# PSUM banks in two halves, first sums evacuated ahead, low-rank product by column halves, and another order of the first loads

One Trainium2 chip, one core. The metric is the device time of that core in microseconds (us): the median of several executions, of which most agree within 0.3%. The span of a trace is about 1.75 us shorter than the time of the same execution (the traced run of the kernel before took 699.6 us and has a span of 697.8), so times are compared with times and spans with spans.

## The reference, cut

```python
def _attn_ref(q, k, v, lam):                     # (4, 8, 768, 64), float32
    for b in range(nb):                          # blocks of the sequence
        intra = (q k^T * decay mask) v           # within the block
        inter = (q * lam^(pos+1)) kv_state       # from earlier blocks
        out[block] = intra + inter
        kv_state = lam^block * kv_state + (k * lam^(block-1-pos))^T v

def _moe_ref(x, U, V, w_ch1, w_ch2):             # x: (4, 768, 512)
    h = x.transpose(0, 2, 1) @ U @ V             # rank 32, mixes tokens
    u = x + h.transpose(0, 2, 1)
    return u + relu(u @ w_ch1) @ w_ch2           # 512 -> 2048 -> 512
```

## The kernel before

The attention runs in 24 steps of 128 tokens (six for each of four batches); `x_nat` is its result, tokens on partitions. When the six steps of a batch are done, `low` and `low_sum` form its low-rank part, `mix` adds it (`pu`), and `turn` transposes the sum (`put`), splits it into parts for the later products, and sends the sum to DRAM (`u_d`; one of the parts has the same name). The tiles with p are PSUM tiles: within a step, `pq` and `pk` hold the transposed q and k, `pss` the scores, `px` the weighted v, `pkv` the new state, `pxn` the transposed result; `pp` and `pr` belong to the low-rank product. Each is emptied by an instruction on ScalarE or VectorE (the copies `qt`, `kt`, `xt`, `x_nat`, for instance), and the program gives its bank to the next tile only after that. `mask` holds the powers of the decays by which the scores are multiplied (`sm`). In the head, the first units of products, the last `mix` and `turn` pieces stand between the products. After that come only products: `pz` takes two of the three parts of a product, `pd` the third.

```python
    x_pool = mix_ctx.enter_context(tc.tile_pool(name="x", bufs=8, side="right"))
    ...
    ps = ctx.enter_context(tc.tile_pool(name="ps", bufs=8, space=bass.MemoryType.PSUM))
    def bank(shape, name):
        return ps.tile(shape, FP32, tag="bank", name=name)      # one ring of eight banks
    ...
    def back(s):                       # end of step s: transpose the attention's result
        px = bank([P, CT, P], "pxn")
        for ct in range(CT):
            nc.tensor.transpose(out=px[:, ct, :], in_=xt[:, ct, :], identity=ident)
        xs[s] = x_pool.tile([P, C], FP32, tag="x", name="x_nat")
        nc.scalar.copy(xs[s].rearrange("p (c n) -> p c n", n=P), px)

    def low(b):                        # 12 records: column groups 0..3, then 0..1
        pp = bank([P, C], "pp")
        for c in range(NT):
            g = c % G
            nc.tensor.matmul(
                out=pp[g * R : (g + 1) * R, :], lhsT=u_w[:, c, :], rhs=xs[b * NT + c],
                start=(c < G), stop=(c + G >= NT),
            )
        pts[b] = tmp("pt")
        nc.scalar.copy(pts[b], pp)

    def mix(s):
        pu = bank([P, C], "pu")
        nc.tensor.matmul(out=pu, lhsT=v_hl[:, c * P : (c + 1) * P], rhs=p_hl, start=True, stop=True)
        nc.vector.tensor_tensor(out=xs[s], in0=pu, in1=xs[s], op=ALU.add)

    def turn(s):
        pt = bank([P, CT, P], "put")
        ...
        nc.sync.dma_start(out=u_d[s], in_=xs.pop(s))   # in the attention steps: one step later
    ...
    load_next("q")                     # step 0 in two halves each
    load_next("k", nc.scalar)
    nc.scalar.dma_start(out=lamb, in_=lam.unsqueeze(0).broadcast_to([P, H]))   # the decays
    for name in "vqkvqkv":
        load_next(name)
    ...
    def hidden(ft, pair, before={}):   # one unit of products
        ...                            # 16 pz, then 8 pd, with pieces of mix and turn between
        for g in pair:
            pz, pd = acc[g]
            r = r_pool.tile([P, N], FP32, tag="r", name="r")
            nc.scalar.mul(r, pz, 1.0 + E)
            nc.vector.scalar_tensor_tensor(r, pd, 4096.0, r, ALU.mult, ALU.add)
            nc.sync.dma_start(out=r_d[ft][g], in_=r)
```

## Time and profile before

| | |
|---|---|
| time, median of 3 (range) | 700.29 us (699.34 to 700.83) |
| span of the trace | 697.8 us |
| TensorE busy | 684.1 us, 98% |
| VectorE, ScalarE, GpSimd busy | 72%, 44%, 15% |
| moved by DMA | 131.18 MB, mean 188 GB/s |

TensorE leaves 13.7 us of the span idle. Every part of the change can only win from these or from work on TensorE before 171 us. The prediction shows the views that say where they lie.

### The profile page before, as it was taken

To read this page: it belongs to the slowest core of one execution; us is meant where nothing else is said; L and a number is where in the kernel's file an instruction comes from. 1 tells how busy PE (TensorE), PEld (TensorE's weight loads), DVE (VectorE), ACT (ScalarE), POOL (GpSimd) and SP (SyncE) were. 2 spreads that over 40 slices of the span, in tenths; PEclk is the share of its full clock that TensorE was granted. 3 is DMA by queue.
4 is the path that set the end of the run, shared out by engine and by line. 5 is a ranking of instruction groups with operands and counts; after the bars stand their busy time and mean duration, and the time that the engine had idled before them with its cause. 6 is when DMAs were issued, how large, how long until landed. Compare 5 with 4: busy or idle time off the path is not lost.

```text
span 697.8 us, 11361 instructions
## 1 busy us (share of the span) xinstructions
PE 684.1 (98%) x4176; PEld 555.3 (80%) x4176; DVE 501.5 (72%) x903; ACT 305.6 (44%) x543; POOL 108.0 (15%) x91
## 2 busy tenths in 40 slices
PE   7999999998999999999999999999999999999997
PEld 6979797966888888888888888888888888888886
DVE  4868787866899777777779435777686586776864
ACT  4777777854566544444455322232232222322320
POOL 3425554524000000000000000011030030300300
PEclk9999999999999999999999999999999999999999
DMA  9997786333477555656657889966354363363531
GB/s 196 219 200 183 181 212 166 95 101 141 170 258 250 197 203 211 209 208 209 206 204 269 288 304 366 351 193 201 96 163 150 90 212 99 122 187 90 167 92 60
DMA packets 131688, 131.18 MB, mean 188 GB/s; under 512 B 81392, under 2 KB 89584, under 8 KB 131632
## 3 DMA queue, kind: packets, MB, share of 16 engines
q1 hardware_dynamic: 130432, 130.18, 61.1%
q8 instruction: 33, 0.54, 0.3%
q10 hardware_dynamic: 1200, 0.27, 0.2%
q14 instruction: 23, 0.19, 0.1%
HBM read 80.09 MB, written 50.33 MB: 187 GB/s over the span
## 4 chain that ended last, share of the span: by engine, by line
PE 88%; DVE 4%; ACT 3%; DMA 2%; issue 1%; POOL 0%; ACTq 0%; DVEq 0%; POOLq 0%
PE pz L613 25%; PE pz L745 13%; PE pz L743 13%; PE pd L747 13%; PE pd L620 12%; PE pss L341 2%; PE px L364 2%; PE px L359 2%; DMA u_d<-x_nat 2%; PE pxn L404 1%; PE put L456 1%; PE pkv L380 1%; DVE ut L460 1%; PE pk L306 1%; PE pq L306 1%
## 5 line engine op out<-in xcount | busy, mean ns | idle before, releaser
L613 PE MATMUL pz<-u_hl,w 128*128 128x512 f32 x768 | 190.4, 398 | 0.0
L613 PEld LDWEIGHTS pz<-u_hl,w 128*128 128x128 f32 x768 | 144.5, 188 | 36.0 <-issue 1.3
L743 PE MATMUL pz<-w_hl,m 128*128 128x512 f32 x384 | 151.6, 396 | 0.0
L745 PE MATMUL pz<-w_hl,m 128*128 128x512 f32 x384 | 151.6, 396 | 0.0
L747 PE MATMUL pd<-w_d,m 128*128 128x512 f32 x384 | 150.0, 396 | 0.0
L727 ACT ACTIVATE m<-mt 128x512 fp32r<-128x512 f32 x96 | 60.7, 632 | 196.0 <-PE pd L747 138.2
L728 DVE SCALAR_TENSOR_TENSOR m<-rm,m 128x512 fp32r<-128x512 f32 x96 | 71.5, 746 | 54.3 <-ACT m L727 53.8
L628 DVE SCALAR_TENSOR_TENSOR r<-pd,r 128x512 f32<-128x512 f32 x96 | 61.9, 686 | 59.6 <-ACT r L627 52.5
L767 POOL TENSOR_TENSOR o<-o,u 128x512 f32<-128x512 f32 x20 | 29.9, 1526 | 450.7 <-DVE o L765 450.7
L620 PE MATMUL pd<-u_d,w 128*128 128x512 f32 x384 | 98.8, 397 | 0.0
L745 PEld LDWEIGHTS pz<-w_hl,m 128*128 128x128 f32 x384 | 72.3, 188 | 17.7
L747 PEld LDWEIGHTS pd<-w_d,m 128*128 128x128 f32 x384 | 72.3, 188 | 17.6
L743 PEld LDWEIGHTS pz<-w_hl,m 128*128 128x128 f32 x384 | 72.3, 188 | 17.6
L620 PEld LDWEIGHTS pd<-u_d,w 128*128 128x128 f32 x384 | 72.2, 188 | 17.4
L627 ACT ACTIVATE r<-pz 128x512 f32<-128x512 f32 x96 | 52.0, 594 | 60.8 <-PE pz L613 60.8
L729 DVE SCALAR_TENSOR_TENSOR m<-m 128x512 fp32r<-128x512 f32 x96 | 69.2, 721 | 0.9
L726 DVE TENSOR_SCALAR mt<-rm 128x512 uint32<-128x512 uint32 x96 | 46.2, 482 | 25.3 <-DMA rm<-r_d 25.0
L179 ACT CAST w<-wt 128x512 fp32r<-128x512 f32 x32 | 19.9, 622 | 40.6 <-DVE wt L176 32.4
L364 PE MATMUL px<-sm,vraw 128*64 128x128 f32 x384 | 36.1, 274 | 0.3 <-DVE sm L347 0.2
L347 DVE TENSOR_TENSOR sm<-pss,mask 128x512 f32<-128x512 f32 x48 | 30.9, 685 | 6.2 <-PE pss L341 4.3
L359 PE MATMUL px<-qs,kv 128*64 128x128 f32 x320 | 32.2, 279 | 0.0
L136 ACT ACTIVATE sc<-sc,ends 128x512 f32<-128x512 uint32 x29 | 21.0, 724 | 19.2 <-DVE sc L132 19.2
(82 smaller groups left out, 760.8 us busy)
## 6 DMA issues: line engine op xcount, KB each, us to landing
r_d<-r SPq DMA_DIRECT2D x96, 256.0 KB, 2.8
rm<-r_d SPq DMA_DIRECT2D x96, 256.0 KB, 2.7
words<-in_moe_w_ch_dram SPq DMA_DIRECT2D x32, 512.0 KB, 4.4
w_d<-w SPq DMA_DIRECT2D x16, 768.0 KB, 3.3
w_hl<-w_d SPq DMA_DIRECT2D x16, 512.0 KB, 6.1
u_d<-x_nat SPq DMA_DIRECT2D x24, 256.0 KB, 3.8
u<-u_d SPq DMA_DIRECT2D x24, 256.0 KB, 4.1
out_dram<-o SPq DMA_DIRECT2D x24, 256.0 KB, 2.0
```

The costliest lines, as they stand in the source:

```text
L364: nc.tensor.matmul(out=px[x * D : (x + 1) * D, a, :], lhsT=vr[:, 2 * a + x, :], rhs=sm[:, x, a, :], start=(c == 0), stop=True,)
L613: nc.tensor.matmul(out=acc[g][0], lhsT=w[:, n, ct, :], rhs=uhl[g][:, n, ct, :], start=(ct == 0 and n == 0), stop=(ct == CT - 1 and n == 1),)
L620: nc.tensor.matmul(out=acc[g][1], lhsT=w[:, 2, ct, :], rhs=ud[g][:, ct, :], start=(ct == 0), stop=(ct == CT - 1),)
L627: nc.scalar.mul(r, pz, 1.0 + E)
L628: nc.vector.scalar_tensor_tensor(r, pd, 4096.0, r, ALU.mult, ALU.add)
L726: nc.vector.tensor_scalar(t.bitcast(U32), r.bitcast(U32), HI, None, ALU.bitwise_and)
L727: nc.scalar.activation(out=m[:, 0], in_=t, func=AF.Relu)
L728: nc.vector.scalar_tensor_tensor(m[:, 1], r, 0.0, hi, ALU.max, ALU.subtract)
L729: nc.vector.scalar_tensor_tensor(m[:, 2], hi, E, low, ALU.mult, ALU.subtract)
L743: nc.tensor.matmul(out=pz, lhsT=m[:, 0, cols], rhs=hl[:, 0], start=first, stop=False)
L745: nc.tensor.matmul(out=pz, lhsT=m[:, 1, cols], rhs=hl[:, 1], start=False, stop=end)
L747: nc.tensor.matmul(out=pd, lhsT=m[:, 2, cols], rhs=dd, start=first, stop=end)
```

## The change

Its intent: give `pss`, `px` and `pkv` (and `pz`, `pd` in the first units) PSUM banks of their own; evacuate `pz` while `pd` is still computed; let the second round of the low-rank product use all four column groups of the array; fetch the decays before anything else and the second q and k before the first v. The diff, cut to its core:

```diff
-    def bank(shape, name):
-        return ps.tile(shape, FP32, tag="bank", name=name)
+    def bank(shape, name, tag="bank"):
+        return ps.tile(shape, FP32, tag=tag, bufs={"bank": 4}.get(tag, 2), name=name)
 # load(): v of step 0 in one piece
-        n = H // parts(s)
+        n = H if name == "v" else H // parts(s)
 # constants(): make_gather() moved here from step 4
-        pss = [bank([P, HP, P], "pss") for x in range(2)]
+        pss = [bank([P, HP, P], "pss", "pz") for x in range(2)]
-        px = bank([P, HP, P], "px")
+        px = bank([P, HP, P], "px", "pd")
-            pkv = bank([P, HP, D], "pkv")
+            pkv = bank([P, HP, D], "pkv", "pd")
 # low(): four of 512 columns, then four of 256 columns in four column groups
+        for i in range(G):
+            c, cols = G + i // 2, slice(i % 2 * half, (i % 2 + 1) * half)
+            nc.tensor.matmul(
+                out=pp[i * R : (i + 1) * R, cols], lhsT=u_w[:, c, :],
+                rhs=xs[b * NT + c][:, cols], start=False, stop=True,
+            )
 # v_steps(): two of the four ScalarE copies of vp a step earlier, two a step later
-    load_next("q")
-    load_next("k", nc.scalar)
     nc.scalar.dma_start(out=lamb, in_=lam.unsqueeze(0).broadcast_to([P, H]))
-    for name in "vqkvqkv":
+    for name, engine in (
+        ("q", nc.sync), ("k", nc.scalar), ("q", nc.sync), ("k", nc.sync), ("v", nc.scalar)
+    ):
+        load_next(name, engine)
+    for name in "vqkv":
         load_next(name)
 # hidden(): after the products pz, before the products pd
+        rs = {g: r_pool.tile([P, N], FP32, tag="r", name="r") for g in pair}
+        for g in pair:
+            nc.scalar.mul(rs[g], acc[g][0], 1.0 + E)
 ... (the weights' steps a step later, sets of pz and pd banks that alternate: cut)
```

More of the change, by code (lines that the diff above doesn't have):

```diff
@@ L264, in constants @@
         make_identity(nc, ident)
+        make_gather()
         for a in range(HP):
@@ L413, in low @@
         pp = bank([P, C], "pp")
-        for c in range(NT):
-            g = c % G
+        for c in range(G):
             nc.tensor.matmul(
-                out=pp[g * R : (g + 1) * R, :], lhsT=u_w[:, c, :], rhs=xs[b * NT + c],
-                start=(c < G), stop=(c + G >= NT),
+                out=pp[c * R : (c + 1) * R, :], lhsT=u_w[:, c, :], rhs=xs[b * NT + c],
+                start=True, stop=False,
+            )
+        half = C // 2
+        assert 2 * (NT - G) == G
+        for i in range(G):
[3 more added lines that the diff above has]
+                rhs=xs[b * NT + c][:, cols], start=False, stop=True,
             )
@@ L533, in five, with high @@
             )
-            for out, rows in parts((0, 2)):
-                nc.scalar.copy(out, t[rows])
+            high(0)
+        def high(g):
+            for out, rows in parts((g,)):
+                nc.scalar.copy(out, st["t"][rows])
         def low(g):
@@ L543, in v_steps @@
         halves = [moe_V[:, half * SH : (half + 1) * SH] for half in range(2)]
-        return weight_steps(dst, halves, SH, 2 * R) + [five, lambda: low(1), lambda: low(3)]
+        return weight_steps(dst, halves, SH, 2 * R) + [
+            five, lambda: low(1), lambda: high(2), lambda: low(3)
+        ]
     u_side = weight_steps(
@@ L553 @@
         (u_side, (-1, 2, 2, 2, 2)),
-        (v_steps(), (0, 3, 3, 4, 4, 5, 5, 6)),
-        (w1_steps(0), (3, 7, 8, 9, 10, 11, 12, 13)),
-        (w1_steps(1), (5, 14, 15, 16, 17, 18, 19, 20)),
-        (w1_2[:4], (15, 21, 22, 23)),
+        (v_steps(), (0, 3, 3, 4, 4, 4, 5, 6, 6)),
+        (w1_steps(0), (3, 7, 8, 9, 10, 12, 13, 14)),
+        (w1_steps(1), (5, 15, 16, 17, 18, 19, 20, 21)),
+        (w1_2[:3], (15, 22, 23)),
     ):
@@ L560 @@
             side.setdefault(n, []).append(step)
-    side[4].append(make_gather)
     def aside(s):
@@ L594, in enter_first_product, with banks @@
         set_ends(r_pool.tile([P, 2], FP32, tag="ends", bufs=1, name="ends"))
-    def banks():
-        return [bank([P, N], name) for name in ("pz", "pd")]
+    def banks(n, other):
+        tags = ("bank", "bank") if other else ("pz", "pd")
+        pzs, pds = ([bank([P, N], name, tag) for i in range(n)] for name, tag in zip(("pz", "pd"), tags))
+        return list(zip(pzs, pds))
+    turns = iter([0, 0, 0] + [1, 0] * (NG * FT))
     def hidden(ft, pair, before={}):
-        acc = {g: banks() for g in pair}
+        acc = dict(zip(pair, banks(len(pair), next(turns))))
         count = iter(range(12 * len(pair)))
@@ L624, in hidden @@
         for g in pair:
-            pz, pd = acc[g]
-            r = r_pool.tile([P, N], FP32, tag="r", name="r")
-            nc.scalar.mul(r, pz, 1.0 + E)
-            nc.vector.scalar_tensor_tensor(r, pd, 4096.0, r, ALU.mult, ALU.add)
-            nc.sync.dma_start(out=r_d[ft][g], in_=r)
+            nc.vector.scalar_tensor_tensor(rs[g], acc[g][1], 4096.0, rs[g], ALU.mult, ALU.add)
+            nc.sync.dma_start(out=r_d[ft][g], in_=rs[g])
     def w2_steps(ft):
@@ L679 @@
     head = [(pair, ft) for two in (pairs[:2], pairs[2:]) for ft in (0, 1) for pair in two]
-    side = list(zip((2, 3, 3, 4), w1_2[4:]))
+    side = list(zip((2, 2, 3, 3, 4), w1_2[3:]))
     for i, (pair, ft) in enumerate(head):
@@ L732 @@
     acc = {}
+    spare = next(turns)
     def product(i, n, parts=range(3)):
@@ L737, in product @@
         if ft == 0:
-            acc[n] = banks()
+            acc[n] = banks(1, n // 2 != spare)[0]
         pz, pd = acc[n]
```

## The prediction

> **What bounds the kernel now.** I read the busy row by slices first, then the chain that ended last, then the waits of TensorE, and only then the timeline in the places those three point to.
>
> ```profile
> PE   7999999998999999999999999999999999999997
> ...
> PE pz L613 25%; PE pz L745 13%; PE pz L743 13%; PE pd L747 13%; PE pd L620 12%; PE pss L341 2%; PE px L364 2%; PE px L359 2%; DMA u_d<-x_nat 2%; PE pxn L404 1%; PE put L456 1%; PE pkv L380 1%; DVE ut L460 1%; PE pk L306 1%; PE pq L306 1%
> ```
>
> TensorE is busy from end to end, and three quarters of the chain are the products pz and pd of the two matrix stages. The chain in order of time shows how full that part is:
>
> ```profile
> 171.06 3.75 PE pz L613 x16
> 174.82 1.87 PE pd L620 x8
> 176.69 3.75 PE pz L613 x16
> ```
>
> Sixteen products of 512 columns take 3.75 us, eight take 1.87: 234 ns each, without a gap, from 171 us to about 690 us. Nothing in the change removes a product there, so those 519 us cannot move; the old eight banks already hide every evacuation. Whatever the change is worth lies in 0 to 171 us and must be an idle stretch of TensorE or work taken from it. Those are:
>
> ```profile
> 1.85 4.36 DMA lamb<-in_lam_dram
> 6.30 2.65 DVE mask L268 x8
> 8.95 0.02 issue
> 8.98 0.17 DVE small L272
> 9.15 1.20 DVE sm L347 x2
> 10.35 0.04 issue
> 10.39 0.93 PE px L364 x13
> ```
>
> The start waits for the decays (lamb), not for q and k: they land at 6.2 us, then eight scans and the masking run.
>
> ```profile
> 38.38 0.66 PE L404 MATMUL pxn<-ident,xt 128*128 128x128 f32 x4 [1.18 <-ACT xt L369]
> ```
>
> One gap of 1.18 us at 38 us: the chain shows ScalarE making four copies of vp (0.52 us each, 35.65 to 37.73) ahead of xt, after VectorE spent 30.14 to 31.67 us on gather.
>
> ```profile
> 156.98 0.63 PE L456 MATMUL put<-ident,x_nat 128*128 128x128 f32 x4 [0.86 <-ACT uf L467]
> 159.88 0.63 PE L456 MATMUL put<-ident,x_nat 128*128 128x128 f32 x4 [0.41 <-ACT uf L467]
> ...
> 166.61 0.63 PE L456 MATMUL put<-ident,x_nat 128*128 128x128 f32 x4 [1.24 <-ACT uf L467]
> ...
> 169.51 0.63 PE L456 MATMUL put<-ident,x_nat 128*128 128x128 f32 x4 [0.41 <-ACT uf L467]
> ```
>
> Four gaps, 2.92 us together, where the first units of products are mixed with the last transposes. The profile blames uf, but x_nat (the addition on VectorE) ends at 156.84, 0.14 us before the transpose: the true recurrence is transpose, ut, u_d, x_nat, next transpose, 2.90 us a turn, and before 156.98 and 166.61 VectorE also did the two evacuations r.
>
> **What the Trainium skill says.**
> - Perfetto Trace Analysis, Optimizing Tensor Performance, Matmuls: groups should rotate through different PSUM banks so that evacuation overlaps the next products. The trace agrees with eight (no gap after 171 us). The change gives the attention part a rotation of four, so this is where to look for harm.
> - TensorEngine Tiling (Array Packing), Key Properties: independent tiles of the array run in parallel, and 128x32 gives four. The trace agrees: the twelve records of pp, 512 columns each, take 1.84 us in the chain, while pk, four transposes of 128 columns over the whole array in the same fp32, takes 0.44 us for those 512 columns in a pass. Twelve in a row would be 5.3 us; 1.84 is about two rounds of two passes (1.76).
> - PSUM, Terms: two engines on one bank at once are an error, reads included. The trace agrees in that uf begins 0.18 us after u_d, its neighbour on the same bank, has ended. So a bank is held until its last reader in turn.
> - DMA: Bandwidth & Descriptors, Specifications: below 512 B a transfer is not at line rate. All 12,430 packets of the first 16 us are smaller, and after a burst of up to 281 the rate stays at 204 to 222 GB/s, where later slices of the page reach 366.
>
> **The change part by part.**
>
> *Start.* The decays are asked for first, and gather moves into the time when VectorE waits for them. The mask should be done near 7 us rather than 8.95. But TensorE runs in order, and the transposes of the second q and k stand before px. In the old trace the second k is transposed at 9.02 us. Its data come fifth of five loads of 256 KB; now v of the first step goes on ScalarE's queue, but it shares the same saturated transfers, so about as many bytes precede the second k, and it lands near 8.9. px then starts near 9.5 instead of 10.39: **-0.9 us**. A third load ahead is still deep enough afterwards (5 us to land, nearly 15 us of lead).
>
> *v.* gather (1.5 us of VectorE) is gone from there, and two of the four vp copies come a step earlier, two a step later. The gap of 1.18 goes, perhaps 0.05 stays: **-1.15 us**.
>
> *Low rank.* Round two used two of the four column groups for 512 columns; now four groups take 256 columns each. It falls from 2 x 0.44 to 2 x 0.22: some 0.43 us, four times: **-1.7 us**. All four stand on TensorE's path.
>
> *First sums ahead.* The copies pz to r (2 x 0.54 on ScalarE) now run beside pd's products (1.87 us), so VectorE's r can begin when pd ends. In the old trace it begins at 153.63, with x_nat before it done at 153.00: about 0.5 us earlier, at 163.26 likewise. Two gaps shrink by 0.5 each: **-1.0 us**. The two of 0.41 stay, as they are the recurrence itself. From 171 us on: 0.
>
> *Banks.* pss, px and pkv keep banks of their own. pq, pk, pu, pxn, put (and pp, pr) share four. In a full step the order on TensorE is pxn, put, pq, pk, pu: pu is the fourth after pxn and gets its bank. The order of the changed program, with its waits, confirms it: every pu of a full step but the first waits for the copy x_nat out of pxn, and two of the four pp wait for the copy qt out of pq. The old program has no such wait. Is x_nat in time? ScalarE holds it back itself, as the buffer it fills is still being written out:
>
> ```profile
> ACT x_nat L406 <- DMA u_d<-x_nat: 8.1, 5, 2.2
> ...
> 63.35 0.48 PE L439 MATMUL pu<-vp 128*128 128x512 f32 x1
> ...
> 63.79 0.59 ACT L406 COPY x_nat<-pxn 128x512 f32<-128x512 f32 x1 [1.29 <-DMA u_d<-x_nat]
> ```
>
> Here pu started 1.03 us before x_nat ended. Over all steps, start of pu against end of x_nat: 63.35 and 64.38; 74.06 and 74.88; 93.17 and 93.97; 104.34 and 105.64; 110.03 and 111.00; 123.52 and 123.94; elsewhere x_nat is first or level. Added up 5.3 us, some 5.8 with 0.07 us for the signal. Not all of it comes: the transfer is sent off after the step's pk, so a stall of one pu gives the next transfer more time, and old waits at 108.31 (0.49) and 114.06 (0.22) are covered by it. I book 1.1 + 0.2 + 0.9 + 0.8 (104 and 110 together) + 0.35 and 0.15 of crumbs: **+3.5 us**.
>
> Sum: -0.9 - 1.15 - 1.7 - 1.0 + 3.5 = -1.25. 700.29 - 1.25 = 699.0; I put the estimate at **698.8 us**, a little lower, because the stalls shrink most easily.
>
> **The rivals.**
> 1. *The new bank wait costs nothing.* If the transfers u_d land sooner, for instance because TensorE's stalls and the other start shift them, only the gains remain: -4.75, 695.5 us. For it: most steps have x_nat level with pu within 0.1 us. Against: five waits with a median landing of 3.9 us and up to 5.1 are in the old trace, and the chain pk, issue, landing, x_nat has nothing in it that the change shortens.
> 2. *The bank wait comes in full*, the stalls not helping the next step, and pp's wait for qt eats what its halves save: +5.8 - 4.75 + 0.5, 701.8 us. For it: at 74 us pp began 0.9 us before qt ended. Against: the argument of the sent-off transfer above.
> 3. *The start does not move*, since the small packets set the landing of the second k: 0.9 us less gain, 699.7. For it: the flat rate of some 218 GB/s. Against: v, which went ahead of the second q and k, now runs beside them.
> 4. *The head gets a wait of its own*: units 0 to 2 all use one set of pz and pd banks, so unit 1 needs ScalarE's two copies done at 152.0, when its first product is due at 152.25 in the old trace. A late copy would cost some 0.3 us twice. A gain of far more than 5 us has no source: there is no more idle time before 171 us to win.
>
> **Range and chances.** The gains are each small and known to about 0.4 us, together some 0.9; the stall is known to about 2. That gives 695.8 to 701.2 for eight in ten. Two per cent are 14 us: faster than 686.3 would need more than all idle time of TensorE (13.7 us of the span, 5 of it at the end and before the first data). Faster 0.01, within 2% 0.98, slower 0.01.
>
> **What would show it right or wrong.** Right: waits of pu for x_nat near 60, 90 and 100 us, none over 1.5 us; pp groups of about 1.4 us; px of the first step near 9.5 us; no gap before pxn at the sixth step; two smaller gaps at the mixed units; 234 ns a product after that. Wrong: pu without a wait for x_nat (rival 1), pu waiting in nearly every step (rival 2), px at 10.4 (rival 3), pz of the second or third unit waiting for r (rival 4), or a product rate other than 234 ns after 171 us, which none of this foresees.

## The result, and the profile after

The changed kernel took **701.77 us** (median of 6, 700.14 to 703.87), the kernel before **700.32** (699.34 to 700.83) in the same rounds: ratio 1.002, 95% interval 1.0002 to 1.0038. By the limit of 2% that is "same". A ratio here is the mean time of one kernel's fast runs over that of the other's of the same rounds, so not quite the ratio of the medians quoted. The predicted range ended at 701.2, so the time lies above it; the class was right.

First the start. The chain that ended last, kernel after (start, length, what):

```profile
1.78 5.80 DMA kraw<-in_k_dram
7.62 0.69 PE pk L308 x2
8.31 2.01 PE pss L343 x16
10.32 0.93 PE pq L308 x4
11.69 1.07 PE px L366 x16
```

The decays no longer stand in the chain; the second half of the first k does, and px is reached at 11.69 us instead of 10.39. (In the kernel before, two of the sixteen px run at 9.80 and the rest from 10.39. A cleaner mark is the first pss of the second step: 13.18 us instead of 11.88.) The busy tenths of the 16 DMA engines and the bytes moved, in each fifth of a microsecond from 0 to 8 us, show why. Before:

```profile
DMA  0000000003658999999999999999999999999999
GB/s 0 0 0 0 0 0 0 0 0 76 145 118 204 286 287 263 271 291 264 229 224 220 220 192 181 226 219 213 222 221 215 221 216 207 219 223 220 219 218 216
```

After:

```profile
DMA  0000000003456235635799999999999999999999
GB/s 0 0 0 0 0 0 0 0 0 91 103 117 129 54 85 115 137 80 128 163 232 248 250 264 265 248 269 268 237 232 223 229 227 219 218 220 216 218 218 218
```

From 2.4 to 3.8 us, where the kernel before moves 204 to 291 GB/s, the changed one moves 54 to 137, and its DMA engines are busy for 2 to 6 tenths of the time only: they are not full.

Then the banks. The waits of TensorE, kernel after (total us, times, longest):

```profile
PE pu L449 <- ACT x_nat L408: 4.0, 3, 1.8
PE put L466 <- ACT uf L477: 2.0, 4, 0.8
PE pxn L406 <- ACT xt L371: 0.4, 1, 0.4
```

The first line has no counterpart before; there the lines (those of the first loads left out) were:

```profile
PE put L456 <- ACT uf L467: 2.9, 4, 1.2
PE pxn L404 <- ACT xt L369: 1.7, 2, 1.2
PE pr L425 <- ACT pt L421: 0.2, 1, 0.2
```

The longest of the waits of pu, and the copy that it waits for, in the timeline:

```profile
113.47 0.59 ACT L408 COPY x_nat<-pxn 128x512 f32<-128x512 f32 x1 [3.41 <-DMA u_d<-x_nat]
114.11 0.49 PE L449 MATMUL pu<-vp 128*128 128x512 f32 x1 [1.75 <-ACT x_nat L408]
```

ScalarE sat idle for 3.41 us because x_nat goes into a buffer that the DMA u_d was still reading; pu then waited 1.75 us for the bank that this copy empties. The other two waits (0.94 at 64.58 us, 1.33 at 95.69) have the same cause.

The gains are there too. One low-rank product, chain of the kernel before and then of the kernel after:

```profile
39.91 1.84 PE pp L416 x12
```

```profile
40.37 1.00 PE pp L417 x8
41.36 0.43 PE pp L426 x8
```

That is 1.84 against 1.43. The waits of put in the head fell from 2.9 to 2.0 us (0.86, 0.41, 1.24, 0.41 became 0.33, 0.40, 0.52, 0.77: the last one grew), and the gap before pxn at the sixth step from 1.18 to 0.39. From the last transposes on the same 16 products take the same 3.75 us:

```profile
173.24 3.75 PE pz L634 x16
```

### The profile page after: what moved, and what is told of

Read it like the earlier page. It is cut to its first block, busy times and chain, and to the rows that moved or that the text cites. A ratio compares the mean times of both kernels' runs of the same rounds, so it can differ in the third digit from the quotient of the medians.

```text
span 700.1 us, 11380 instructions
## 1 busy us (share of the span) xinstructions
PE 683.6 (98%) x4192; PEld 555.9 (79%) x4192; DVE 501.5 (72%) x903; ACT 305.7 (44%) x543; POOL 108.0 (15%) x91
## 4 chain that ended last, share of the span: by engine, by line
PE 91%; DMA 4%; DVE 3%; ACT 1%; issue 0%; ACTq 0%; DVEq 0%
PE pz L634 25%; PE pz L765 13%; PE pz L767 13%; PE pd L769 13%; PE pd L644 13%; PE pss L343 3%; DMA u_d<-x_nat 3%; PE px L366 2%; PE px L361 2%; PE pxn L406 1%; PE pkv L382 1%; PE put L466 1%; PE pq L308 1%; PE pk L308 1%; DMA kraw<-in_k_dram 1%; DVE sm L349 1%
```

## The experiments

Fifteen kernels ran. All outputs are right. Each batch shared a chip and its runs of the kernel before (medians 700.25, 700.01, 700.23 and 700.23 us). "After" is the changed kernel. What a part costs is read below from the difference of two ratios. Their intervals reach 0.0012 to 0.0018 to either side, so such a difference is uncertain by some 0.002, or 1.5 us (an estimate from these intervals).

### What the banks cost: one ring again, and nine buffers

e1 is after with all eight banks in one ring:

```diff
-        return ps.tile(shape, FP32, tag=tag, bufs={"bank": 4}.get(tag, 2), name=name)
+        return ps.tile(shape, FP32, tag="bank", bufs=8, name=name)
```

> The changed kernel with one ring of eight banks again, everything else kept. Theory (ring): the four-bank ring makes pu wait for the copy x_nat, 4.0 us of waits in the trace and some 4.3 us between 44 us and 142 us once the two shorter pp are counted; so this run is 4 us faster than the changed kernel, about 697.7 us and 0.996 of the kernel before, and no pu waits for x_nat. Rival (side work): the attention part is longer because weight conversions were shifted by a step and delay ScalarE; then this run stays within 1 us of 701.8 and the x_nat copies come as late as before, with TensorE waiting elsewhere for them.

Measured: 697.79 us (697.4 to 698.1), ratio to before 0.9967 (0.9955 to 0.998). No pu waits any more. By the two ratios the ring of four costs 1.002 - 0.9967 = 0.0053 of 700.3, that is 3.7 us. The same edit between e2 and e7 (both with the old start, see below) gives 0.9995 - 0.9945 = 0.0050, or 3.5 us. The rival (weights' steps that delay ScalarE) is out: those steps are the same in e1.

e3 leaves the ring of four and gives x_nat a ninth buffer. It has to take one from r, since SBUF is full otherwise:

```diff
-tc.tile_pool(name="x", bufs=8, side="right")
+tc.tile_pool(name="x", bufs=9, side="right")
-tc.tile_pool(name="r", bufs=5, reuse_waits="tile")
+tc.tile_pool(name="r", bufs=4, reuse_waits="tile")
```

> The changed kernel, four-bank ring kept, but with nine instead of eight buffers for x_nat (and four instead of five for r, to fit). Theory (ring and write-out together): x_nat then waits for a write-out issued a step earlier, so it comes at most 0.1 us after the moment at which pu wants its bank; pu's waits vanish though the ring is the same, 3 to 4 us faster than the changed kernel, about 698. Rival (ring alone): ScalarE is too late for a ring of four anyway, waits of the same length stay, time 701.8.

Measured: 697.0 us (696.41 to 697.66), 0.9958 (0.9944 to 0.9972). The waits of x_nat from 30 to 150 us name no transfer any more; kernel after first, then this one:

```profile
ACT x_nat L408 <- DMA u_d<-x_nat: 8.6, 5, 3.4
ACT x_nat L408 <- PE pxn L406: 3.2, 5, 1.1
```

```profile
ACT x_nat L408 <- PE pxn L406: 5.2, 7, 1.1
```

So neither cause is enough for the wait of pu. With four banks and a copy in time pu doesn't wait (e3); with eight banks and a late copy it doesn't either (e1). It takes both: a short ring ties pu to a copy, and a full pool ties the copy to a transfer.

e10 asks whether the ninth buffer is worth something to the kernel before (the same edit on it):

> The kernel before with nine buffers for x_nat (and four for r), nothing else. In the old kernel x_nat also waits for u_d (8.1 us in 5 waits) but pu does not depend on the copy, so those waits are hidden; only a pxn (0.49) and a pr (0.22) were behind them. Theory 'the late write-out costs only through the ring of four': 699.5 us (699.0 to 700.0), ratio 0.998 to 1.000, no waits of x_nat for u_d in the trace. Rival 'the late write-out costs the old kernel too, so the nine buffers are a gain apart from the ring': 697 or less, as with nine buffers in the changed kernel (4.8 less).

Measured: 698.5 us (698.08 to 698.61), 0.9973 (0.9961 to 0.9986), between the two expectations. The late copy cost the old kernel as well, 1.9 us by the ratio and 1.0 by the two traced spans (697.8 and 696.8, the former of a quick run). Of these, the waits of pxn (0.49) and of pr (0.22), which I had called nearly nothing, are gone in the trace. Of the 1.002 - 0.9958 = 0.0062, or 4.3 us, that nine buffers win in the changed kernel, some 1 to 2 us are therefore not the ring's.

### Where the wait goes when one bank is moved

e4 is after with pxn in the pair of banks of px and pkv, so that pu no longer needs the bank of pxn:

```diff
-        px = bank([P, CT, P], "pxn")
+        px = bank([P, CT, P], "pxn", "pd" if s < NS - 1 else "bank")
```

> The changed kernel with pxn moved into the pair of banks of px and pkv, so that the ring of four carries put, pq, pk, pu and the reader that is late, x_nat, holds up pkv instead, which comes some 3 us after pu. Theory (ring): the longest lateness of x_nat seen is 1.8 us, so pkv never waits and the 4 us come back: about 697.7 us, as with one ring of eight. Rival (side work): no change, 701.8.

Measured: 701.47 us (700.12 to 702.02), 1.0018 (1.0006 to 1.0031): nothing won, against my expectation. The waits of TensorE of e4:

```profile
PE pp L417 <- ACT qt L312: 3.4, 2, 1.9
PE pxn L406 <- ACT xt L371: 1.1, 2, 0.7
```

The wait of pu is gone and pp has one instead. pp gets the bank of pq, which is emptied by the copy qt, and qt stands on ScalarE behind the late x_nat (in after, x_nat starts at 113.47 us and qt at 113.95). In after pp has the bank of pq too, as the prediction says, but there pu has already waited for x_nat just before. So freeing TensorE from one late copy leaves it tied to the next copy behind it.

e13 tests that explanation: pp leaves the ring of four too.

```diff
 # on top of e4
-        pp = bank([P, C], "pp")
+        pp = bank([P, C], "pp", "pz" if b < B - 1 else "bank")
```

> The changed kernel with pxn in the pair of banks of px and pkv (as in the run where the wait moved to pp and qt), and pp as well out of the ring of four, in the pair of pss. Theory 'the wait moved because pp, not pu, then took over the bank that a copy behind the late x_nat has to empty': no wait of pp for qt, and pp waits at most for its own data, the last x_nat, some 0.5 us twice: 698.2 us (697.6 to 699.0). Rival 'pxn in that pair costs by itself, or the old start and late x_nat alone explain the 701.5': 700.5 or more, with the 3.4 us of waits found again elsewhere.

Measured: 699.51 us (698.37 to 699.82), 0.9985 (0.9973 to 0.9998). The named wait is gone as the theory has it, but the time lies between the two expectations. Its waits from 30 to 150 us:

```profile
PE pxn L406 <- ACT xt L371: 1.3, 2, 1.0
PE pr L435 <- ACT pt L431: 1.3, 2, 0.9
```

Of the 3.4 us of e4 some 1.5 come back as later waits for ScalarE (2.6 us here against 1.1 for pxn alone in e4). That fits the same late copy passing its delay on, to pt and then to xt; it was not tested by another run.

### What the start costs

e2 is after with the old order of the first loads:

```diff
+    load_next("q")
+    load_next("k", nc.scalar)
     nc.scalar.dma_start(out=lamb, in_=lam.unsqueeze(0).broadcast_to([P, H]))
 ...
+    for name in "vqkvqkv":
```

> The changed kernel with the first loads in the old order (q, k in halves, then the decays, v in halves, then the second q and k), everything else kept. Theory (start): the new order loses 1.35 us at the first px (11.69 against 10.39 us) and nothing makes it up, so this run is some 1.3 us faster than the changed kernel, about 700.4 us, with px at 10.3 and the second half of the first k landing near 5.3 us instead of 7.6. Rival (caught up): a later start only uses up waits that would come anyway (the write-outs land at their own pace), and the time stays at 701.8.

Measured: 699.88 us (699.11 to 700.66), 0.9995 (0.9983 to 1.0008); the first transposes begin at 3.72 us instead of 4.78. By the ratios the new start costs 0.0025 of 700.3, 1.8 us. The same edit between e1 and e7 gives 0.0022 (1.5 us) and between e3 and e9 0.0030 (2.1 us). The traces show the second step's pss 1.5 us earlier than in after (11.65 against 13.18). Three waits of pu remain (2.9 us together), as they should.

Two changes are in that order: the decays go first, and q, k and v are on other queues. e5 is after with the decays moved behind the two halves of k on ScalarE's queue; e6 is the kernel before with only the decays moved to the head.

```diff
 # e5, on after
-    nc.scalar.dma_start(out=lamb, in_=lam.unsqueeze(0).broadcast_to([P, H]))
 ...
         load_next(name, engine)
+        if name == "k" and engine is nc.scalar:
+            nc.scalar.dma_start(out=lamb, in_=lam.unsqueeze(0).broadcast_to([P, H]))
```

> The changed kernel with the small load of the decays moved behind the two halves of k on ScalarE's queue; the second q and k, and v, stay where the change put them. Theory (small load first): the 4 KB load at the head, one row read 128 times over, keeps the transfers slow, which move 54 to 137 GB/s from 2.4 to 3.8 us where the old order moved 204 to 291; then the rate recovers here to over 200 by 2.6 us, the first q is transposed near 3.8 us instead of 4.8, the first px starts near 10.3, and the time falls by about 1.3 us to 700.4. Rival (two queues full): the second q and k on the other queue take the turn of k's second half; then the rate may recover but that half still lands 1 us or more later than the 5.3 us of the old order, and px stays at 11 or later, 701.8.

> The kernel before with only the small load of the decays moved to the head of ScalarE's queue. Theory (small load first): the rate falls to about 100 GB/s until 3.8 us as in the changed kernel, q and k come about 1 us later, mask is early, px starts at 10.2 to 10.8 and the time stays within 0.5 us of 700.3 or gets worse. Rival (two queues full): the rate is as in the old order, the mask is ready 1.8 us earlier, px waits only for the second k at 9.0 us and starts near 9.5: 0.9 us faster, 699.4.

Measured: e5 700.49 us (700.06 to 703.24; two of six runs near 703), 1.0019 (1.0004 to 1.0034); e6 701.06 us (701.04 to 701.5), 1.0019 (1.0006 to 1.0031). The rates from 0 to 8 us of e5, then of e6:

```profile
GB/s 0 0 0 0 0 0 0 0 0 58 79 91 273 284 288 280 280 292 240 227 219 208 192 201 175 179 164 197 222 220 247 252 248 237 232 224 223 218 218 217
```

```profile
GB/s 0 0 0 0 0 0 0 0 1 2 1 82 115 132 125 134 145 181 243 242 284 284 277 275 255 232 225 216 218 220 216 219 201 210 214 227 216 223 222 210
```

The slow stretch goes with the decays and not with the queues: it leaves the changed kernel when they move back and appears in the old one when they move forward. e6 shows that the one move alone makes the old kernel slower, by 1.3 us (0.4 to 2.2). Little of that is seen at the start itself: the second step's pss begins at 12.02 instead of 11.88, and pr waits 1.0 us for ScalarE instead of 0.2; the rest was not located. In e5 the first px begins at 10.08 (before: 9.80) and the second step's pss at 12.16 (before: 11.88; after: 13.18): most of the loss is gone, but not all, as px now waits for a mask that is late. The time of e5 doesn't show this gain: its ratio is that of after. Two of its six runs were near 703, for which I have no trace.

The decays are one row of 32 bytes, read 128 times: 4 KB in 128 packets. e14 keeps them first on the same queue but loads the row once and spreads it by a product with ones:

```diff
-    nc.scalar.dma_start(out=lamb, in_=lam.unsqueeze(0).broadcast_to([P, H]))
+    nc.scalar.dma_start(out=lam_row, in_=lam.unsqueeze(0))          # [1, H]
 ...
+    nc.vector.memset(ones, 1.0)                                     # [1, P]
+    pl = bank([P, H], "pl")
+    nc.tensor.matmul(out=pl, lhsT=ones, rhs=lam_row, start=True, stop=True)
+    nc.vector.tensor_copy(out=lamb, in_=pl)
```

> The changed kernel, the decays still first on ScalarE's queue, but as one row of 32 bytes, spread over the partitions by a product with ones on TensorE. Theory 'the 128 packets of the small load slow the transfers behind it': the rate before 4 us goes back to 270 to 290 GB/s, the first transposes at 3.8 instead of 4.8, the first px near 9.5 instead of 11.7, and 699.9 us (the changed kernel less 1.9). Rival 'anything first on that queue delays k': first pq still after 4.5, px after 11, 701.5 or more.

Measured: 697.63 us (695.84 to 698.02), 0.9957 (0.9944 to 0.9971): 4.4 us less than after by the ratios, more than the 1.9 expected, and by more than the uncertainty. The first transposes begin at 3.13 us and px at 9.40. The rates from 0 to 8 us:

```profile
GB/s 0 0 0 0 0 0 0 0 0 90 177 261 204 156 156 195 224 188 236 215 174 252 271 270 275 283 283 288 291 287 289 293 287 286 291 286 288 287 247 251
```

Two things are to be seen. The slow stretch is milder (156 to 236 instead of 54 to 137), as the theory of the 128 packets has it, though not back at the 204 to 291 of before. And later the rate stays near 285, where every kernel with the broadcast settles near 218. The transfers u_d became faster too: their median time from issue to landing between 40 and 150 us is 3.4 us, 3.8 in after, and in the traced run, the fastest of the five, pu waits only once, for 0.51 us. So part of the extra gain is the bank wait that shrinks.

The second point is not evidence about the small packets. From 8 to 24 us the profile has these lines for SyncE's queue (packets, MB, share of 16 engines' span), before and then e14:

```profile
q1 hardware_dynamic: 12367, 3.29, 122.8%
q1 hardware_dynamic: 14309, 3.78, 102.7%
```

That is 1.228 x 16 x 16 us / 12367 = 25.4 ns a packet against 18.4: the loads of q, k and v, in packets of 256 bytes, each took longer. In the packet records they take 18 ns at first in every kernel and grow longer later in all but e14 and e15. In e5 they do so from 3.6 us on (23.4 ns on average from 3.6 to 4.2), while the first packet of the decays moves only at 4.26. So the decays' packets had not moved yet when the loads slowed. e14 and e15 share a second change that was not meant: the two new tiles (32 and 512 bytes a partition) stand in front of the buffers of q, k and v and shift them by 544 bytes. The kernel before, after and e16 have the first of these buffers at byte 124128 of a partition and e14 and e15 at 124672, which is a multiple of 256. Whether the addresses, the missing broadcast or something else keeps the packets short, and how much of the 4.4 us goes with it, no run separates; a run with the broadcast and the shifted buffers would.

### Do the parts add up, and what is best

e7 is after with both harmful parts undone (the edits of e1 and e2). e9 has the edits of e2 and e3: the old start and nine buffers, with the ring of four kept.

> The changed kernel with one ring of eight banks and with the old order of the first loads: what is left is the low-rank part by halves, the first sums ahead, and the spread of v's copies and gather. If the parts add up: 697.8 (one ring) less 1.9 (what the old order of loads gained in the run before) = 695.9 us, 0.994 of the kernel before. Rival (parts overlap: an earlier start runs into later waits for the write-outs): 697 or more.

> The changed kernel with nine buffers for x_nat (four for r) and the old order of the first loads; the ring of four banks stays. If the two faults are independent: 697.0 less 1.9 = 695.1 us, 0.9927 of the kernel before, the best so far, and no pu waits for x_nat. Rival (overlap): 696.5 or more.

Measured: e7 695.88 us (695.43 to 696.82), 0.9945 (0.9933 to 0.9957); e9 694.79 us (694.71 to 695.06), 0.9928 (0.9916 to 0.994). Both are where the single effects, added, put them. By the ratios e9 beats before by 5.0 us and after by 6.4.

e15 is e9 with the row of e14 first on ScalarE's queue; e16 is e9 with the broadcast kept, but first on GpSimd's queue.

> The version with nine buffers and the old start, with the decays as one row first on ScalarE's queue. The mask is then ready long before px, and px waits for the transposes of the second k alone, near 9.2 to 9.6 instead of 10.2: 694.1 us (0.7 less than without). If the row delays the queue as the broadcast did: 695.6 or more.

> The same with the broadcast of 128 small packets kept, but first on GpSimd's queue, and q and k first on their own queues. If the packets slow all queues' transfers: rate under 200 GB/s before 3.5 us, first pq after 4.4, 695.6 us or more. If only what stands in the same queue behind them is slowed: first pq at 3.8 and 694.1 us.

Measured: e15 694.48 us (694.2 to 695.11), 0.9918 (0.9904 to 0.9932); e16 695.09 us (694.37 to 695.77), 0.9925 (0.9912 to 0.9937). Neither is told apart from e9 by its interval. In e15 px begins at 10.03, not at the 9.2 to 9.6 expected, and not before the 9.69 of e9: the transposes of the second q and k before it took 1.9 us (8.13 to 10.03), where e14 needed 1.0 (8.37 to 9.40); the runs don't say why. Its loads run as fast as those of e14, and no gain over e9 shows from that either. In e16 nothing is slowed (the first transposes begin at 3.71, 251 to 288 GB/s from 2.4 to 3.6 us). It is no clean test of the queue, though, as GpSimd's queue shows 32 packets there and not 128.

### What the other gains are worth alone

e11 is before with only `low` by column halves, e12 is before with only the copies of pz ahead of pd, in one ring of eight banks. Their edits are those parts of the diff above.

> The kernel before with only the low-rank product by column halves. If the 0.41 us that pp loses in the trace of the changed kernel is worth as much in the old one, four times: -1.6 us, 698.6 us. If pp's later half then waits for x_nat (the last x_nat of the batch is the copy that is held up), less than half of it: 699.4 or more.

> The kernel before with only the copies of pz into r ahead of the products pd, all eight banks in one ring. By the gaps before put in the changed kernel's trace: -0.9 us, 699.3 us, gaps before put of 0.3 to 0.8 instead of 0.86, 0.41, 1.24, 0.41; 234 ns a product after the head. Rival: gain from having two own sets of banks in the head, so nothing here: 700.2.

Measured: e11 698.72 us (698.39 to 699.15), 0.9978 (0.9965 to 0.9992), which is -1.5 us (-0.6 to -2.5); e12 698.71 us (698.24 to 699.35), 0.9978 (0.9966 to 0.9991), -1.5 us (-0.6 to -2.4). In e11 the faster pp meets a new wait of pr for ScalarE's copy of it, 1.3 us in two; the time fell all the same, in part because the 0.49 before pxn is gone. In e12 the waits of put from 150 to 175 us are:

```profile
PE put L456 <- ACT uf L467: 1.7, 4, 0.5
```

That is 1.2 us less than the 2.9 of before, so the rival (a gain from having two sets of banks) is refuted; the rest of the 1.5 is within the spread of the runs.

## Why the prediction was right or wrong

| term | predicted | measured | from |
|---|---|---|---|
| start | -0.9 | +1.8 | after against e2, ratios |
| v | -1.15 | -0.8 | the gap before pxn, traces (no run of its own) |
| low rank | -1.7 | -1.5 | e11 |
| first sums ahead | -1.0 | -1.5 | e12 |
| banks | +3.5 | +3.7 | after against e1, ratios |
| sum | -1.25 | +1.7 | measured as a whole: +1.4 (0.002 of 700.3) |

**The start** is the step that failed. It was said as "it shares the same saturated transfers, so about as many bytes precede the second k, and it lands near 8.9". The mask was indeed early (ready at 7.06 us instead of 8.95), and that half of the step held. But the step took for granted that the transfers stay saturated when 4 KB move to the front, and that the second k is the last thing px waits for. The rate fell to some two fifths for 1.4 us (54 to 137 against 204 to 291 GB/s), with the DMA engines busy for 2 to 6 tenths. This delayed the second half of the first k (transposed at 7.62 instead of 5.35 us), the scores after it, and with these px; the second q and k, transposed after the scores, waited for no data. e5 and e6 tie the fall in rate to the one load. That its 128 packets are the reason is supported by the milder stretch in e14 but not shown, since e14 changed more than the packets; and why the DMA engines stand idle there is open. The size of the whole term, 1.5 to 2.1 us by three pairs of runs, is shown. The miss of this term, 1.8 + 0.9 = 2.7 us, is nearly the whole distance between 698.8 and 701.8.

**The banks** held in mechanism and in size. pu waits for x_nat, because x_nat waits for u_d: e1 takes the ring away, e3 the late copy, and each ends the wait. That the sum came so close is in part luck: the prediction booked stalls at six or more places, the largest 1.1 us, and the trace has three, of 0.94, 1.33 and 1.75 us. Two more details were off. I said no wait would pass 1.5 us, and the longest is 1.75. And I took the waits of the old kernel for hidden except for 0.7 us, while e10 wins 1 to 2 us there.

**Low rank** and **first sums** held. pp fell by 0.41 us where 0.43 was predicted, and the put gaps of 0.86 and 1.24 fell by 0.53 and 0.72 where 0.5 each was predicted. That both count in full in the changed kernel is not shown by its trace alone: the last put gap, which was to stay at 0.41, grew to 0.77. **v** left a wait of 0.39, not 0.05: pxn still waits for xt there. The late phase is unchanged, as predicted. One reading of the prediction is off, without consequence: uf begins 0.11 us after u_d has ended (156.24 and 156.35 us); the 0.18 is how long ScalarE had been idle.

**The rivals.** Rival 2 (the bank wait comes in full, 701.8) hit the time, but not by its reasons: the bank wait came at 3.7 and not at 5.8, and pp's wait for qt shows no gap of TensorE in the changed kernel (at 114.60 us pp follows pu at once); it appears in e4. Rival 3 (the start does not move) was the nearest to the point and still too kind; a start that becomes worse was not among the rivals at all. Rivals 1 and 4 are refuted: pu waits three times, and no unit in the head waits for r.

## What to carry to other kernels

Splitting a ring of banks by tag makes each part shorter. Before doing it, ask for each tile which copy empties the bank that it will now get, and what that copy itself waits for; one spare buffer further down was worth as much here as four banks more (e3 and e1, not told apart by their intervals), and moving a single tile may only hand the wait to the next copy in the same engine's order. A small load is not free to move: at the head of the queue, these 4 KB in 128 packets cost more by what they held up than their early arrival was worth, so look at the rate in the first microseconds and not only at which load the chain names. A test that adds a tile also moves the tiles behind it: compare the addresses before a difference is put down to the edit that was meant. When gains and losses of a change nearly cancel, run its parts alone: here two parts were worth 1.5 us each and the best mixture (694.8 us) beats both kernels.

## What the Trainium skill lacked or had wrong

- DMA: Bandwidth & Descriptors, section Issuing engines are not separate DMA queues, says that transfers of all issuing engines run on the same 16 DMA engines and interleave. The traces agree: the decays on ScalarE's queue delayed q on SyncE's queue (first transposes at 4.62 instead of 3.86 us in e6). The page does not say that a load of 4 KB made of one short row read 128 times can hold the transfers beside and behind it to 54 to 137 GB/s for 1.4 us (after; e6 82 to 181).
- The same page, section Specifications: the prediction used its limit of 512 B to explain the flat 218 GB/s. In e14 all packets before 8 us are still smaller than 512 B and the rate is near 285, so packet size alone was not the reason. What was is open (25.4 against 18.4 ns a packet, before and e14).
- Perfetto Trace Analysis, section Matmul Optimizations, advises to use all eight PSUM banks. Both kernels do; in the changed one, with the eight divided into 2, 2 and 4, pu waited 4.0 us in the trace, and 3.7 us went with the division (e1). The page does not speak of how the banks are divided.
